# First pair's queries and the gates on ScalarE's queue, one transpose for the tails of keys and queries, and a new task order

## The chip, the core and the metric

One Trainium2 chip, one core. The metric is the device time of one execution of the whole program, in microseconds, as the median of several runs. A profiled execution gives the trace that is read below.

## What is computed

Attention with a memory, then two feed-forward layers, all in float32:

```
scores = q k^T / 8, causal; a = softmax(scores); local = a v            # B 4, H 8, S 576, D 64
q_p = phi(q) = max(q, 0) + exp(min(q, 0))
mem = (q_p M_prev) / (q_p . z_prev + 1e-6)
g = sigmoid(beta) per head;  x = g * mem + (1 - g) * local              # -> 2304 tokens x 512
x = (silu(x W_gate) * (x W_val)) W_out                                   # inner width 1536
out = m(x W_in) W_out2,  m = 0, h or (h + 1)^2 / 4 by the value of h     # inner width 2048
```

## The kernel before

Heads are taken two at a time: 16 pairs, numbered 0 to 15, four per batch. A pair's 576 positions are four chunks of 128 and a tail of 64. Each pair goes through the same tasks. Its keys (tile kn), queries (qn) and values (vn) are loaded; TensorE turns the keys (task tk for the chunks, tm for the tails of keys and queries) and the queries (tq); ScalarE copies the turned tiles from PSUM (to KK, SZ or SX, and QZ or Q4 for the tails). The scores of a head follow (qk0 and qk1 by head, qk4 for the tails of both heads, in two halves), VectorE takes mask and maximum (mx), ScalarE the exponential with its sum (ex), VectorE inverts the sums (sum, tile r), GpSimd scales the rows (.sc), TensorE turns them (t03, t02, t01, t4 for the first head and the tails, t13, t12, t11 for the second), ScalarE or VectorE copies them (R), and TensorE forms the products with the values and the memory (av00 to av11). Beside that runs the memory path: ScalarE's two passes over qn (tile e), VectorE's p, GpSimd's w, fold and pn, the turn tp and its copy PP. The result x is stored to a scratch tensor xs.

The pairs of the first batch use plain float32 matmuls. From pair 4 on each operand is split into a high and a low part; ScalarE writes the high part, VectorE the low one, and SyncE copies the turned keys to the other half of the partitions (task dup, KK<-KK), which the scores wait for.

In between, TensorE has filler work: 72 blocks of six matmuls (mm<-xh,wu) that already form the first layer's inner products for three groups of 512 tokens and six slices of 256 columns, as soon as their x and the decoded weights are there. Twelve units of weights are decoded in this part as well (raw, wA, wS, wu; ScalarE, VectorE and GpSimd). Their results go out as gvo.

The order of all this on each engine is fixed when the program is built. `Plan.order` is a list scheduler: each task has an engine, an estimated duration and a priority, and a free engine takes the ready task with the lowest priority for which buffers are free. For a pair's task the priority is 100 times the pair's number plus an entry of the table `ORDER`; `EARLY` holds the priorities of the weight units, `GROUP_AT` and `X_AT` those of the filler's groups and of their loads. PSUM has five banks for the attention and three for the filler. SyncE issues nearly all transfers, in order. From the end of the filler on, a second plan runs the two layers; its priorities are other numbers, which the change doesn't touch.

At the start, `Attention.__init__` builds masks, gates and zeroed tiles; `pair` then adds the tasks. The lines that matter are those of the loads (`l_k`, `l_q`), `tm` and its copies:

Of the kernel before, what the change touches and what calls it, by code (L numbers as in the profile page):

```python
# [18 lines left out]
P = 128  # L19
# [18 lines left out]
EARLY = (-695.6332, 2783.9892, 1285.5157, 4826.1976, -587.204, 1099.0329, 1783.7958, 812.7126, 3810.6396, 6743.5654, -296.1106, 490.4918)  # L38
# [4 lines left out]
GROUP_AT, X_AT = (38662.3623, 35325.2542, 46229.556), (412.8002, 381.1663, 182.3662)  # L43
# [16 lines left out]
    "load": -940.6324, "load_v": 203.5903, "load_z": -887.0432, "load_M": -747.8821, "tk": -333.4689, "tm":  # L60
    -812.4048, "tk.hi": -890.2619, "tm.hi": 1721.9097, "tq": 461.8326, "tq.hi": 1307.1915, "min": 1423.9267,
    "exp": 311.185, "phi": 204.0583, "w": -1122.4349, "fold": -293.9033, "nrm": -731.8656, "pn": 1733.8628,
# [9 lines left out]
    -1003.2927, "M_lo": 15.9112, "tk.lo": 391.3507, "tm.lo": -125.9973, "dup": -273.878, "tq.lo": 560.4026,  # L72
# [159 lines left out]
def c_tr(n):  # L232
    return 109 * n
# [39 lines left out]
class Attention:  # L273
# [3 lines left out]
    def __init__(self, ctx, tc, plan, q, k, v, M_prev, z_prev, beta, cst, xs):  # L277
# [17 lines left out]
        ac = self.ac  # L295
        self.mask0 = ac.tile([P, 512], F32, name="mask0")
# [12 lines left out]
        bb = ac.tile([P, H], F32, name="bb")  # L309
        nc.sync.dma_start(bb, beta.partition_broadcast(P))  # L310
# [35 lines left out]
        for t in self.kn + self.vn:  # L346
            nc.gpsimd.memset(t[64:128, 4], 0.0)
# [4 lines left out]
        for t in self.SZ + self.QZ + self.MZ:  # L352
            nc.gpsimd.memset(t, 0.0)

    def pair(self, b, n):
# [17 lines left out]
        def add(eng, dur, name, fn, deps=(), uses=(), port=False):  # L373
            t = pl.add(eng, dur, num * 100 + ORDER[name], fn, deps, uses, port=port)
            t["name"] = name
            return t

        def dma(name, times, fn, deps=(), uses=()):
            t = pl.dma(num * 100 + ORDER[name], times, fn, deps, uses)
            t["name"] = pl.last["name"] = name  # L380
            return t
# [34 lines left out]

        def tail_full(t, src):
            nc.sync.dma_start(t[:, 8, :], src.rearrange("h p d -> h p d"))
# [23 lines left out]
        def M_lo():  # L442
            nc.gpsimd.tensor_sub(st["Mhl"][:, :, 1, :], st["mraw"], f32(st["Mhl"][:, :, 0, :]))

        l_k = dma("load", [728, 728, 182], load(
            "kn", lambda: self.kn[i_k.slot], lambda t: t[:, 0:4], self.k, tail_half), uses=[i_k])
        l_q = dma("load", [728, 728, 182], load(
            "qn", lambda: self.ld.tile([P, 9, D], F32, name="qn", tag="qn"), lambda t: t[:, 0:8].rearrange("p (c h) d -> p c h d", h=2), self.q, tail_full),
            uses=[i_q])
# [36 lines left out]
        def tm():  # L486
            t = psum("tm", i_tm)
            nc.tensor.transpose(
                t[:, 0:128], st["kn"][:, 4].rearrange("p h d -> p (h d)"), self.ident)
            nc.tensor.transpose(t[0:64, 128:256], st["qn"][:, 8], self.ident)  # L490
# [9 lines left out]
        t_tm = add("PE", c_tr(2), "tm", tm, [l_k, l_q], [i_k, i_q, i_tm, i_Q4] + i_K)  # L500
# [8 lines left out]
        if exact_q:  # L509
            t_k = copies("tk", [(lambda: st["tk"], lambda: f32(mk_K(0)[:, 0, 0:512]), 512)], [t_tk], [i_tk, *i_K])  # L510
            t_Q4 = copies("tm", [(lambda: st["tm"][:, 0:64], lambda: f32(mk_K(0)[:, 0, 512:S]), 64)] + [
                (lambda h=h: st["tm"][up, 128 + h * 64:192 + h * 64], lambda h=h: QZ[halves[h], h], 64)
                for h in range(2)], [t_tm], [i_tm, i_Q4, *i_K])
            t_K = [[t_k, t_Q4]] * 2
        else:
            t_k = [split("tk", k_parts("tk", slice(0, 512), slice(0, 512), h), [t_tk], [i_tk, i_K[h]], 100) for h in range(2)]
            tails = [x for h in range(2) for x in k_parts("tm", slice(0, 64), slice(512, S), h)]
            for h, j in ((0, 0), (1, 3)):
                tails.append((lambda h=h: st["tm"][up, 128 + h * 64:192 + h * 64],
                              lambda j=j: Q4[up, j], lambda j=j: Q4[dn, j], 64))  # L520
# [859 lines left out]
```

## Time and profile before

| | |
|---|---|
| median of three runs | 1110.57 us (1105.44 to 1111.51) |
| the profiled execution | 1110.57 us, of which 1108.8 us are its span, first to last instruction |
| TensorE busy | 1076.6 us (97%), 5520 matmuls |
| VectorE, ScalarE, GpSimd busy | 756.6, 565.4, 257.0 us |
| last product of the attention part, next stage's first matmul | 347.4 us, 360.0 us |

A busy time is the union of an engine's instructions; matmuls are pipelined, so a matmul's duration is longer than the step from its start to the next one's. PEclk is the clock that TensorE was granted, as a share of 2.4 GHz. The idle time in brackets behind a row is what the engine stood still before it, and what ended that.

### The profile page before, as it was taken

What the parts mean: (1) busy time and instruction counts of PE and PEld (TensorE: products, weight loads), DVE (VectorE), ACT (ScalarE), POOL (GpSimd) and SP (SyncE); (2) the same over time, 40 slices, a digit from 0 to 9 for tenths busy, and PEclk for the clock granted to TensorE, in tenths of its full rate; (3) what the DMA queues carried; (4) which work ended last, traced back from release to release, by engine and by line L of the source; (5) the groups of instructions that cost most, each with busy time, mean ns of one, the idle gap of its engine ahead of it and who ended that gap; (6) DMA issues with size and microseconds to landing.
All of it is one profiled execution on the core that took longest, in us unless ns stands there. A gap on an engine that the chain in (4) does not pass through costs nothing.

```text
span 1108.8 us, 16480 instructions
## 1 busy us (share of the span) xinstructions
PE 1076.6 (97%) x5520; PEld 924.7 (83%) x5520; DVE 756.6 (68%) x1699; ACT 565.4 (51%) x1286; POOL 257.0 (23%) x325
## 2 busy tenths in 40 slices
PE   6997999999999999999999999999999999999998
PEld 4565788888888998888789997888888888889997
DVE  5688989888983788798945559999433443343433
ACT  6888889999884254544433334454222222222222
POOL 6898669666653000000000000000000000000000
PEclk9999999999999999999999999999999999999999
DMA  5567545765725889976635567361300110110000
GB/s 138 156 172 187 146 123 150 209 165 127 234 91 173 289 302 320 345 235 202 212 104 176 166 221 246 111 236 57 110 1 1 57 39 1 43 39 1 29 1 29
DMA packets 148325, 156.42 MB, mean 141 GB/s; under 512 B 70160, under 2 KB 109072, under 8 KB 148240
## 3 DMA queue, kind: packets, MB, share of 16 engines
q1 hardware_dynamic: 147664, 154.31, 44.8%
q8 instruction: 44, 0.72, 0.3%
q10 hardware_dynamic: 576, 1.05, 0.2%
q14 instruction: 41, 0.34, 0.1%
HBM read 105.78 MB, written 42.47 MB: 134 GB/s over the span
## 4 chain that ended last, share of the span: by engine, by line
PE 50%; DVE 1%; DMA 0%; issue 0%; ACT 0%; DVEq 0%
PE acc L1274 27%; PE mm L1036 23%; DMA ys<-yo 0%; DVE t L1238 0%; DVE h L1251 0%; DVE wA L956 0%; DVE t L1244 0%; DVE wu L984 0%; DVE wA L977 0%; ACT yo L1304 0%; DVE yo L1308 0%; DVE wS L961 0%; DVE wA L949 0%; DVE wA L952 0%; ACT oo L1340 0%
## 5 line engine op out<-in xcount | busy, mean ns | idle before, releaser
L1036 PE MATMUL mm<-xb,wu 128*128 128x512 f32 (+1 forms) x1968 | 410.7, 363 | 0.0
L1036 PEld LDWEIGHTS mm<-xb,wu 128*128 128x128 f32 x1968 | 357.4, 188 | 42.0 <-DVE t L1242 0.2
L1274 PE MATMUL acc<-wu,h 128*128 128x512 f32 x864 | 208.1, 390 | 0.0
L1274 PEld LDWEIGHTS acc<-wu,h 128*128 128x128 f32 x864 | 161.8, 188 | 32.3
L1248 ACT CAST h<-t 128x512 fp32r<-128x512 f32 (+1 forms) x140 | 80.9, 578 | 180.6 <-DVE t L1242 90.1
L1274 PE MATMUL acc<-h,wu 128*128 128x512 f32 (+1 forms) x720 | 152.6, 368 | 2.4 <-DVE h L1251 2.4
L1236 DVE SCALAR_TENSOR_TENSOR t<-t 128x512 f32<-128x512 f32 (+1 forms) x80 | 51.0, 638 | 146.9 <-ACT t L1230 146.9
L1274 PEld LDWEIGHTS acc<-h,wu 128*128 128x128 f32 x720 | 131.0, 188 | 20.5 <-DVE h L1251 3.7
L1251 DVE TENSOR_TENSOR h<-t,h 128x512 fp32r<-128x512 f32 (+1 forms) x140 | 89.0, 636 | 71.8 <-ACT h L1248 71.5
L1230 ACT ACTIVATE t<-mm,half 128x512 f32<-128x512 f32 (+1 forms) x80 | 51.5, 644 | 147.6 <-PE mm L1036 147.2
L1036 PE MATMUL mm<-xh,wu 128*128 128x512 f32 x432 | 115.0, 405 | 1.2 <-DMA xh<-xs 0.9
L755 POOL TENSOR_SCALAR a<-a,r,OGP 128x256 f32<-128x256 f32 (+3 forms) x144 | 96.1, 680 | 28.1 <-DVE r L746 9.7
L1036 PEld LDWEIGHTS mm<-xh,wu 128*128 128x128 f32 x432 | 77.4, 190 | 16.1 <-DMA xh<-xs 1.8
L677 ACT ACTIVATE a<-a,mn 128x128 f32<-128x128 f32 (+3 forms) x128 | 71.0, 558 | 12.7 <-DVE mn L670 12.3
L981 ACT CAST wu<-wA 128x512 fp32r<-128x512 f32 x64 | 39.7, 620 | 52.9 <-DVE wA L977 52.3
L944 ACT ACTIVATE wA<-raw 128x512 f32<-128x512 f32 x64 | 43.2, 675 | 45.3 <-DVE wu L984 20.6
L1082 ACT COPY gvo<-mm 128x512 f32<-128x512 f32 (+1 forms) x80 | 42.9, 544 | 41.3 <-PE mm L1036 40.9
L670 DVE CUSTOM_DVE_ANT_0 a<-s,mask 128x256 f32<-128x256 f32 (+3 forms) x128 | 57.7, 484 | 7.2 <-PE s L664 4.8
L397 DVE TENSOR_TENSOR R<-t,R 128x384 fp32r<-128x384 f32 (+3 forms) x120 | 53.3, 484 | 4.5 <-ACT R L393 3.7
L956 DVE SCALAR_TENSOR_TENSOR wA<-raw,wA 128x512 uint32<-128x512 uint32 x68 | 54.3, 801 | 0.6
L1242 DVE TENSOR_TENSOR t<-t,mm 128x512 f32<-128x512 f32 (+1 forms) x80 | 50.6, 632 | 2.2
L664 PE MATMUL s<-KK,SX 128*128 128x512 f32 (+3 forms) x192 | 42.0, 342 | 8.3 <-DMA KK<-KK 3.5
(134 smaller groups left out, 1401.5 us busy)
## 6 DMA issues: line engine op xcount, KB each, us to landing
raw<-in_moe_w_out_dram SPq DMA_DIRECT2D x28, 512.0 KB, 4.5
xb<-xs SPq DMA_DIRECT2D x24, 512.0 KB, 6.2
gv<-gv SPq DMA_DIRECT2D x24, 512.0 KB, 4.4
gv<-gvo SPq DMA_DIRECT2D x44, 256.0 KB, 4.6
xs<-x SPq DMA_DIRECT2D x16, 576.0 KB, 3.3
raw<-in_moe_w_in_dram SPq DMA_DIRECT2D x16, 512.0 KB
KK<-KK SPq DMA_DIRECT2D x24, 288.0 KB
raw<-in_moe_w_gate_dram SPq DMA_DIRECT2D x12, 512.0 KB, 4.7
```

The lines of the kernel that those rows point to most:

```text
L397: nc.vector.tensor_sub(lo(), src(), f32(hi()))
L670: nc.vector.tensor_tensor_reduce(a, st[f"s{h}{c}"][:, 0:kl], self.mask0[:, 512 - kl:512], -0.125, 3.0e38, ALU.add, ALU.min, mn[:, o:o + 1])
L677: nc.scalar.activation(a, a, AF.Exp, bias=mn[:, o:o + 1], scale=-1.0, accum_out=sm[:, o, 0:1])
L755: nc.gpsimd.tensor_scalar(a, a, st["mn"]["r"][:, o:o + 1], self.OGP[:, n, o:o + 1], op0=ALU.mult, op1=ALU.mult)
L956: nc.vector.scalar_tensor_tensor(s["F"], words(s["raw"])[:, :, 1], 0xC0000000, s["A"], op0=ALU.bitwise_and, op1=ALU.bitwise_or)
L1036: nc.tensor.matmul(out, kt_of(unit, pw, kt), x[kt][:, px, cols], start=(kt == 0 and i == 0), stop=(kt == KT - 1 and i == 2))
L1230: nc.scalar.activation(s["t"], src[0][0](), AF.Relu, bias=half, scale=0.5)
L1236: nc.vector.scalar_tensor_tensor(s["t"], s["t"], 1.0, s["t"], op0=ALU.min, op1=ALU.mult)
L1242: nc.vector.tensor_max(s["t"], s["t"], src[0][0]())
L1248: nc.scalar.copy(s["h"][:, 0], s["t"])
L1251: nc.vector.tensor_sub(s["h"][:, 1], s["t"], f32(s["h"][:, 0]))
L1274: nc.tensor.matmul(state[m][:, 0:o], l, r, start=(f == 0 and i == 0), stop=(f == F - 1 and i == 2), skip_group_check=True)
```

## The change

Five things change.

- The first pair's queries (three transfers) and the gates' vector `bb` are issued by ScalarE at the very start; before, SyncE issued them, `bb` ahead of the first keys.
- With each pair's keys the tail of its queries is loaded as well, into the 64 rows of `kn` that were zeroed before (`tail_two`, one more transfer for each pair). The query tile still gets its own copy of the tail, for the memory path.
- `tm` is one transpose of 128 x 128 in place of two, and no longer depends on the load of the queries. The copies read the queries' tail from columns 64 to 127; for a split pair the second head's high part now lies in the lower half of the partitions.
- The zeroing of SZ, QZ and MZ moves from GpSimd to VectorE, that of kn's unused rows goes.
- `ORDER`, `EARLY`, `GROUP_AT` and `X_AT` hold new numbers, so the tasks of the attention part stand in another order on every engine.

```diff
-EARLY = (-695.6332, 2783.9892, 1285.5157, 4826.1976, ...
+EARLY = (-287.4065, 1887.8432, 16137.615, 9256.0877, ...
-GROUP_AT, X_AT = (38662.3623, 35325.2542, 46229.556), (412.8002, 381.1663, 182.3662)
+GROUP_AT, X_AT = (20260.1724, 25727.3732, 55014.2119), (875.5215, -266.6973, -218.444)
...
-    "load": -940.6324, "load_v": 203.5903, "load_z": -887.0432, "load_M": -747.8821, "tk": -333.4689, "tm":
+    "load": -1161.5582, "load_v": 452.1889, "load_z": -1110.878, "load_M": 414.315, "tk": -2068.1283, "tm":
...
+        bb = ac.tile([P, H], F32, name="bb")
+        self.q0 = self.ld.tile([P, 9, D], F32, name="qn", tag="qn")
+        for h in range(2):
+            nc.scalar.dma_start(self.q0[:, 0:8].rearrange("p (c h) d -> p c h d", h=2)[:, :, h, :],
+                                q[0, h, 0:512, :].rearrange("(c p) d -> p c d", p=P))
+        nc.scalar.dma_start(bb, beta.partition_broadcast(P))
+        nc.scalar.dma_start(self.q0[:, 8, :], q[0, 0:2, 512:S, :].rearrange("h p d -> h p d"))
...
-        bb = ac.tile([P, H], F32, name="bb")
-        nc.sync.dma_start(bb, beta.partition_broadcast(P))
...
-        for t in self.kn + self.vn:
+        for t in self.vn:
             nc.gpsimd.memset(t[64:128, 4], 0.0)
...
-        for t in self.SZ + self.QZ + self.MZ:
-            nc.gpsimd.memset(t, 0.0)
+        for t in self.QZ + self.SZ + self.MZ:
+            nc.vector.memset(t, 0.0)
...
+        def tail_two(t, src):
+            tail_half(t, src)
+            nc.sync.dma_start(t[dn, 4], self.q[b, hs, 512:S, :].rearrange("h p d -> p h d"))
...
+        if near:
+            l_q = add("DMA", 1820, "load", lambda: st.update(qn=self.q0), [], [i_q])
+        else:
+            l_q = dma("load", [728, 728, 182], load(
...
-            nc.tensor.transpose(t[0:64, 128:256], st["qn"][:, 8], self.ident)
...
-        t_tm = add("PE", c_tr(2), "tm", tm, [l_k, l_q], [i_k, i_q, i_tm, i_Q4] + i_K)
+        t_tm = add("PE", c_tr(1), "tm", tm, [l_k], [i_k, i_tm, i_Q4] + i_K)
...
-                (lambda h=h: st["tm"][up, 128 + h * 64:192 + h * 64], lambda h=h: QZ[halves[h], h], 64)
+                (lambda h=h: st["tm"][halves[h], 64:128], lambda h=h: QZ[halves[h], h], 64)
```

How the engines' rows move, at three places. Lines of the new kernel are 11 to 12 higher behind the inserted code.

ScalarE, from its first instruction to its first exponential of scores, before (e is the memory path's pass over the queries, KK, QZ and SZ the copies that the first scores read):

```order
L313 ACT_TABLE_LOAD
L313 ACTIVATE gate<-bb 128x8
L316 ACTIVATE ogate<-bb 128x8
L505 COPY KK<-tk 128x512
L552 ACTIVATE e<-qn 128x576
L505 COPY KK<-tm 128x64
L505 COPY QZ_180<-tm 64x64 x2
L555 ACTIVATE e<-e 128x576
L505 COPY SZ_178<-tq 64x512 x2
L717 ACTIVATE a_0_170,sum_156<-a_0_170,mn 128x576
```

And now:

```order
L299 DMA qn<-in_q_dram 128x4x64 x2
L301 DMA bb<-in_beta_dram 128x8
L302 DMA qn<-in_q_dram 128x1x64
L318 ACT_TABLE_LOAD
L318 ACTIVATE gate<-bb 128x8
L321 ACTIVATE ogate<-bb 128x8
L563 ACTIVATE e<-qn 128x576
L516 COPY SZ_180<-tq 64x512
L566 ACTIVATE e<-e 128x576
L516 COPY SZ_180<-tq 64x512
L516 COPY KK<-tm 128x64
L516 COPY QZ_182<-tm 64x64 x2
```

Four transfers stand ahead of the table load, and the copy of the keys' chunks (KK<-tk), which was the first copy, is the last of them, behind the twelve rows shown.

TensorE in pair 7, before: the last twelve rows of the stretch from the turn of its keys (tk, with the seven rows of a product av00 behind it) to its first score (s<-KK,SX):

```order
L863 MATMUL av_2000<-R_1730,vhl 128x64
L533 MATMUL tq<-ident,qn 128x128 x4
L802 MATMUL t_2031<-ident,a_1743 128x128 x4
L802 MATMUL t_2040<-ident,a_1814 128x128 x4
L1036 MATMUL mm<-xh,wu 128x512 x6
L802 MATMUL t_2067<-ident,a_1871 128x128 x3
L819 MATMUL t_2073<-ident,a_1761 128x128
L819 MATMUL t_2073<-ident,a_1732 128x128 x2
L802 MATMUL t_2079<-ident,a_1812 128x128 x3
L1036 MATMUL mm<-xh,wu 128x512 x6
L664 MATMUL s_2100<-KK,SX 128x512 x2
L664 MATMUL s_2106<-KK,SX 128x384 x2
```

The same stretch now, from the turn of the tails on (tm, one row), its first twelve rows:

```order
L500 MATMUL tm<-ident,kn_171 128x128
L1047 MATMUL mm<-xh,wu 128x512 x6
L495 MATMUL tk<-ident,kn_171 128x128 x4
L602 MATMUL tp<-ident,p 128x128 x4
L605 MATMUL tp_1873<-ident,p 64x128
L813 MATMUL t_1881<-ident,a_1534 128x128 x3
L544 MATMUL tq<-ident,qn 128x128 x4
L1047 MATMUL mm<-xh,wu 128x512 x12
L675 MATMUL s_1937<-KK,SX 128x384 x2
L1047 MATMUL mm<-xh,wu 128x512 x6
L874 MATMUL av_1958<-PP,Mhl 128x256
L874 MATMUL av_1958<-R_1654,vhl 128x256
```

Behind these there follow the other three rows of that product, t4 (5 transposes), six filler matmuls, t01 (3 transposes) and a product of 256 columns, and then pair 7's first score; s_1937 is pair 6's. Twenty-four filler matmuls lie between the turn and the score, where there were twelve.

TensorE at the end of the attention part, before: the last product of pair 15, the filler behind it and the next stage (mm<-xb,wu):

```order
L863 MATMUL av_5070<-R_4968,vhl 128x64
L863 MATMUL av_5070<-R_4969,vhl 128x320 x3
L863 MATMUL av_5070<-R_4969,vhl 128x192
L863 MATMUL av_5070<-R_4969,vhl 128x64
L1036 MATMUL mm<-xh,wu 128x512 x54
L1036 MATMUL mm<-xb,wu 128x384 x384
```

And now:

```order
L813 MATMUL t_5071<-ident,a_4920 128x128 x3
L1047 MATMUL mm<-xh,wu 128x512 x12
L874 MATMUL av_5094<-PP,Mhl 128x320
L874 MATMUL av_5094<-R_5004,vhl 128x320 x3
L874 MATMUL av_5094<-R_5004,vhl 128x192
L874 MATMUL av_5094<-R_5004,vhl 128x64
L874 MATMUL av_5094<-R_5005,vhl 128x320 x3
L874 MATMUL av_5094<-R_5005,vhl 128x192
L874 MATMUL av_5094<-R_5005,vhl 128x64
L1047 MATMUL mm<-xh,wu 128x512 x36
L1047 MATMUL mm<-xb,wu 128x384 x384
```

Three of the nine filler blocks behind the last product have moved ahead of it.

## Rows read from the trace of the kernel before

**Rows 1.** The page's first line.

```profile
span 1108.8 us, 16480 instructions
```

**Rows 2.** Busy us of each engine by stretch (x: instructions), granted clock, DMA share, GB/s.

```profile
0.00:20.00 20.00, 13.18 (x56) 9.01 (x56) 10.01 (x46) 12.74 (x32) 13.38 (x38) 1.00 0.51 123
20.00:100.00 80.00, 73.24 (x379) 49.18 (x380) 61.92 (x178) 69.92 (x196) 70.43 (x76) 0.98 0.65 172
...
160.00:345.00 185.00, 181.08 (x1163) 160.67 (x1162) 160.24 (x486) 168.84 (x464) 129.48 (x161) 1.00 0.55 155
...
362.00:1108.80 746.80, 740.02 (x3542) 647.26 (x3540) 470.42 (x848) 261.18 (x459) 0.00 (x0) 1.00 0.40 132
```

**Rows 3.** Whom TensorE waited for, 20 to 345 us: total, times, longest.

```profile
PE s L664 <- DMA KK<-KK: 3.5, 3, 2.5
PE s L664 <- DVE mn L670: 3.1, 2, 2.9
PE av L863 <- ACT PP L505: 2.1, 1, 2.1
PE t L819 <- POOL a L755: 1.7, 1, 1.7
PE s L664 <- DVE R L397: 1.6, 2, 1.4
```

**Rows 4.** One of the three stretches at half clock, as in rows 2.

```profile
155.20:158.60 3.40, 3.40 (x11) 3.02 (x12) 2.06 (x9) 1.36 (x5) 0.01 (x1) 0.50 0.02 6
```

**Rows 5.** Timeline of SyncE's queue at the start: start, length, what.

```profile
4.15 0.64 SPq L418 DMA_DIRECT2D qn<-in_q_dram  x1
```

**Rows 6.** Timeline of ScalarE at the start.

```profile
7.33 0.68 ACT L552 ACTIVATE e<-qn 128x576 f32<-128x576 f32 x1 [1.09 <-DMA qn<-in_q_dram]
...
8.01 0.42 ACT L505 COPY QZ<-tm 64x64 f32<-64x64 f32 x2
...
9.04 1.17 ACT L505 COPY SZ<-tq 64x512 f32<-64x512 f32 x2
```

**Rows 7.** Timeline of TensorE at the start.

```profile
4.53 1.09 PE L483 MATMUL tk<-ident,kn 128*128 128x128 f32 x4 [4.53 <-DMA kn<-in_k_dram]
...
7.26 0.42 PE L490 MATMUL tm<-ident,qn 128*64 128x128 f32 x1 [1.43 <-DMA qn<-in_q_dram]
...
15.55 0.60 PE L533 MATMUL tq<-ident,qn 128*128 128x128 f32 x4
```

**Rows 8.** Timeline of TensorE in pair 7, turn of the keys and first score.

```profile
145.53 0.65 PE L483 MATMUL tk<-ident,kn 128*128 128x128 f32 x4
...
155.19 2.56 PE L664 MATMUL s<-KK,SX 128*128 128x512 f32 x8 [2.46 <-DMA KK<-KK]
```

**Rows 9.** End of the attention part: TensorE, SyncE, and the loads' median time to landing.

```profile
347.39 12.79 PE L1036 MATMUL mm<-xh,wu 128*128 128x512 f32 x54
360.02 3.31 PE L1036 MATMUL mm<-xb,wu 128*128 128x384 f32 x18
...
354.73 0.36 SPq L1110 DMA_DIRECT2D xb<-xs  x1
...
xb<-xs SPq DMA_DIRECT2D x16, 384.0 KB, 5.6
```

**Rows 10.** Timeline of TensorE in a regular pair, the turns of the tails.

```profile
249.44 0.27 PE L488 MATMUL tm<-ident,kn 128*128 128x128 f32 x1
249.55 0.27 PE L490 MATMUL tm<-ident,qn 128*64 128x128 f32 x1
249.58 0.39 PE L863 MATMUL av<-PP,Mhl 128*128 128x320 f32 x1
```

**Rows 11.** Timeline of TensorE, last scores and second head's first turn, pairs 11 and 7.

```profile
243.30 0.57 PE L664 MATMUL s<-KK,SX 128*128 128x256 f32 x4
...
251.54 0.60 PE L802 MATMUL t<-ident,a 128*128 128x128 f32 x4
...
171.85 0.42 PE L664 MATMUL s<-KK,SX 128*128 128x128 f32 x2
...
177.68 0.55 PE L819 MATMUL t<-ident,a 128*128 128x128 f32 x3 [0.54 <-DVE R L397]
```

More of the change, by code (lines that the diff above doesn't have):

```diff
@@ L37 @@
 CUTS = (0, 2, 4)
-EARLY = (-695.6332, 2783.9892, 1285.5157, 4826.1976, -587.204, 1099.0329, 1783.7958, 812.7126, 3810.6396, 6743.5654, -296.1106, 490.4918)
+EARLY = (-287.4065, 1887.8432, 16137.615, 9256.0877, -215.5057, 4250.8554, 811.5698, -202.2738, 4594.4235, 9367.785, 2548.5565, -122.2052)
 XH, GVO = 4, 3
@@ L59 @@
 ORDER = {
-    "load": -940.6324, "load_v": 203.5903, "load_z": -887.0432, "load_M": -747.8821, "tk": -333.4689, "tm":
-    -812.4048, "tk.hi": -890.2619, "tm.hi": 1721.9097, "tq": 461.8326, "tq.hi": 1307.1915, "min": 1423.9267,
-    "exp": 311.185, "phi": 204.0583, "w": -1122.4349, "fold": -293.9033, "nrm": -731.8656, "pn": 1733.8628,
[9 rows of a table removed]
-    -1003.2927, "M_lo": 15.9112, "tk.lo": 391.3507, "tm.lo": -125.9973, "dup": -273.878, "tq.lo": 560.4026,
[5 rows of a table removed]
+    "load": -1161.5582, "load_v": 452.1889, "load_z": -1110.878, "load_M": 414.315, "tk": -2068.1283, "tm":
+    -3489.133, "tk.hi": 1956.633, "tm.hi": 3325.5154, "tq": 1515.3186, "tq.hi": 58.9504, "min": 813.3241, "exp":
[10 rows of a table added]
+    "M_lo": 207.2265, "tk.lo": 630.5307, "tm.lo": -58.8903, "dup": -146.9326, "tq.lo": 1568.2686, "tp.lo":
[4 rows of a table added]
 }
@@ L443, in M_lo @@
             nc.gpsimd.tensor_sub(st["Mhl"][:, :, 1, :], st["mraw"], f32(st["Mhl"][:, :, 0, :]))
[L445 to L449, printed above, removed]
+        l_k = dma("load", [728, 728, 182, 182], load(
+            "kn", lambda: self.kn[i_k.slot], lambda t: t[:, 0:4], self.k, tail_two), uses=[i_k])
+        if near:
+            l_q = add("DMA", 1820, "load", lambda: st.update(qn=self.q0), [], [i_q])
+        else:
+            l_q = dma("load", [728, 728, 182], load(
+                "qn", lambda: self.ld.tile([P, 9, D], F32, name="qn", tag="qn"), lambda t: t[:, 0:8].rearrange("p (c h) d -> p c h d", h=2), self.q, tail_full),
+                uses=[i_q])
         l_v = dma("load_v", [728, 728, 182], load(
@@ L518, in pair @@
             for h, j in ((0, 0), (1, 3)):
-                tails.append((lambda h=h: st["tm"][up, 128 + h * 64:192 + h * 64],
-                              lambda j=j: Q4[up, j], lambda j=j: Q4[dn, j], 64))
+                tails.append((lambda h=h: st["tm"][halves[h], 64:128], lambda h=h, j=j: Q4[halves[h], j],
+                              lambda h=h, j=j: Q4[halves[1 - h], j], 64))
             t_Q4 = split("tm", tails, [t_tm], [i_tm, i_Q4] + i_K)
```

28 rows, old and new, of the table ORDER are left out of this document.

## Prediction

> **What bounds the kernel now.** I read the page first. The span is 1108.8 us [rows 1] inside an execution of 1110.57 us, which is also the median of the three runs, so the sum below is made on 1110.57 and needs no correction between the two. Then the table of stretches [rows 2]. From 362 us on TensorE is busy 740.0 of 746.8 us: it is the bound there, and the two programs hold the same instructions in the same order from that point. The time can therefore only change by moving the end of the attention part, some 360 us. In that part TensorE is busy 13.2 of the first 20 us, 73.2 of the next 80 and 181.1 of the 185 from 160 to 345; ScalarE is busy 168.8 of those 185. So two engines are nearly full, and a saved wait of TensorE is worth its length only while ScalarE keeps up.
>
> Third, who TensorE waits for after the first 20 us [rows 3]: the copy of the keys to the other half of the partitions (KK<-KK) 3.5 us in three waits, score banks that VectorE has not emptied (mn, R) 3.1 and 1.6, ScalarE's copy PP 2.1, the scaling on GpSimd 1.7. Fourth, the clock: after the longest such waits it is granted at 0.50, so at 1.2 instead of 2.4 GHz, for one stretch of 3.4 us [rows 4]; there are three of these (near 22, 111 and 155 us), each after TensorE had stood for 1.7 to 2.9 us. At half speed 3.4 us do the work of 1.7.
>
> **The change part by part.** *The first pair's queries on ScalarE's queue.* Before, their tail is the seventh transfer of SyncE's queue, issued at 4.15 for 0.64 us [rows 5], and TensorE sees it at 7.26 after waiting 1.43 us [rows 7]; it needs 2.5 us from the issue's end to use. In the new order ScalarE issues four transfers first. An issue costs 0.36 us (row of xb, [rows 9]) to 0.64; from about 0.7 us the tail is issued by 2.2 to 3.3 and there by 4.7 to 5.8. That looks like 1.5 to 2.5 us gained. But the copies that the scores need stand on ScalarE behind it in this order: e (0.68), a query copy, e again (0.68), the second query copy (1.17 for the two), the keys' tail and two tail copies (0.42 for the two, and a shorter one that I take at 0.2), the keys (0.58, as one of the two 512-column copies) [rows 6]: 3.7 us. The scores start at 8.4 to 9.5 plus hand-over. Before, the first transposes take 1.09 us for four and later ones 0.60 [rows 7], so the block of scores that ends at 15.55 begins at half speed, and an earlier start buys mostly slow time. I get an end of 15.2 to 16.1 against 15.55: 0, from -0.4 to +0.6. The gates land and are used under this as well, and the zeroing moves from GpSimd to VectorE, which has no other work before the gates: 0, hidden by the same 3.7 us; without that cover each of the two 1024-column zeroings, the widest of it, would cost some 1.2 us (estimated by columns from the 512-column copies at 0.58).
>
> The Trainium skill ("Trainium Kernel Development and Optimization", Key Constraints) says that DMAs of all issuing queues run on the same 16 engines and interleave, so that issuing from several engines saves only the sequencer's issue time. No row shows two queues at work together here. By that rule the gain at the start is at most some issues of SyncE; by the row of SyncE's tail alone it could be the whole 1.43 us wait. The sum takes neither: ScalarE's own queue of copies ends last.
>
> *One transpose for both tails.* Sixteen transposes go. In a full stretch the one of the queries takes 0.03 us of TensorE's time (249.55 to 249.58), the one of the keys 0.11 (249.44 to 249.55) [rows 10]. So 0.5 to 1.8 us, and I take 1.2. The added SyncE issue per pair costs 0.64 us [rows 5], 15 times 0.64 = 9.6 us of a queue; SyncE mostly waits for buffers ahead of these, and the transpose no longer waits for the whole query tile, so I take 0 here and price the other case below.
>
> *The new order: keys.* The scores of a pair from number 4 on wait for ScalarE's and VectorE's copies and the transfer KK<-KK. In pair 7 TensorE starts the transposes of the keys at 145.53, has work for 7.2 us and waits 2.46 us, until 155.19 [rows 8]: this stretch needs 9.7 us. In the new order there stand between the same two points 24 filler matmuls at 12.63 / 54 = 0.234 us (347.39 to 360.02, [rows 9]) = 5.6; 24 transposes (tk 4, tp 5, t12 3, tq 4, t4 5, t01 3) at 0.11 [rows 10] = 2.6; one score of two times 384 columns and two products of 1024 columns each, at 0.234 for 512, = 0.35 and 0.95. That is 9.5 us, so 0.2 of the 2.46 stay. For pairs 8 to 13 the same count gives 6.7 to 13.9 us of work where before it was 6.1 to 6.6, so the small waits there close too. Of 3.5 us of waits and 1.7 of half clock I take 4.2 as gained; the bounds are 0 and 5.2.
>
> *The new order: the rest.* Pair 3's memory queries were turned right ahead of the products that use them, which is the 2.1 us of PP [rows 3]; now three groups of pair 4's scores, some 1.3 us, stand between: -2.0, from -2.1 to 0. Waits for banks: five banks as before, in another order: 0, from -4.7 to +4.7 (their 3.1 and 1.6 gone, or once more). On the other side some products stand closer behind their last turn than any before (about 0.7 to 1.3 us of work in pairs 1, 3 and 4): +1.5, from 0 to +4.2 (twice the row of PP).
>
> *The end of the attention part.* Before, 54 filler matmuls stand behind the last product, 12.63 us [rows 9]. The last x is stored under them, the load of its part issues at 354.73 and lands 5.6 us later (the median of such loads), 360.3; it is first needed after 15 matmuls of the next stage, about 15 x 0.234 x 384 / 512 = 2.6 us after 360.02, so 2.3 us are spare. Now 36 filler matmuls are left: 18 x 0.234 = 4.2 us less cover. 4.2 - 2.3 = +1.9, from 0 to +4.2.
>
> Sum: 0 - 1.2 - 4.2 - 2.0 + 0 + 1.5 + 1.9 = -4.0, and **1110.57 - 4.0 = 1106.6 us**. The single bounds added up would be far wider than anything likely, since they are independent; three quarters of each end about give -8 and +4 for this case, 1102.5 to 1114.5.
>
> **The rivals.** *Faster by more:* the waits for banks go as well, and with no wait over 1.7 us no half-clock stretch comes. For it: these waits stand next to those of the keys, and the keys' chain gets 2 to 7 us more cover. Price: the five rows of [rows 3] sum to 12.0, of which two thirds go, 8.0; two more stretches of half clock, 3.4; transposes 1.2; against that half of the 1.9 + 1.5 above: -10.9, 1099.7 us. Against it: ScalarE's 168.8 of 185 us leaves at most 16 us in the whole stretch.
>
> *Slower:* the chain of the second head's softmax loses its cover. Place: from a pair's last score to the first turn of the second head, through VectorE, ScalarE, VectorE and GpSimd. Before, a regular pair has 8.2 us between them, 243.30 to 251.54, and no wait at the end [rows 11]. In the new order eight of the twelve later pairs have 4.3 to 6.2 us of TensorE's work there. If the chain needs its 8.2, they lose about 2.5 us each, 20 us, less the 5.4 of transposes and keys: +14.6, 1125 us. Against it: pair 7 had only 5.8 us, 171.85 to 177.68, and waited 0.54 for a bank, not for GpSimd [rows 11]. It decides from a need of about 6.5 us on. A smaller form of the same side: SyncE's 9.6 us of added issues fall on the path of the keys: 1110.57 - 4.0 + 9.6 = 1116.2.
>
> *Nothing that can be measured moves:* the waits close, and ScalarE, 91% busy, ends last instead, so that only the transposes and the end count: 1110.57 - 1.2 + 1.9 = 1111.3.
>
> **How the numbers follow.** Chances: the forecast 0.40, faster by more 0.32, softmax chain 0.13, SyncE's issues 0.06, nothing moves 0.09. A measurement here tells about 0.5% from no change, so 1105.0 to 1116.1 counts as the same. The forecast's own range reaches below 1105.0 with some 0.06 of its chance: faster 0.32 + 0.06 = 0.38. Slower: 0.13 and most of the 0.06 = 0.18. Same: the rest, 0.44. The range holds 8 in 10: from 1095, a little under the faster rival, to 1117, which leaves out most of the softmax chain.
>
> **What would show it.** Right: KK<-KK and PP all but gone from TensorE's waits, two or fewer stretches at 0.50, the block of first scores ending between 15 and 16.5 us, the next stage's first matmul near 356 us. Wrong: waits of turns for GpSimd in pairs 7 to 13 (softmax), keys' loads issued later on SyncE (issues), or a first stage at the same 360 us with other waits.

## The result

The changed kernel takes 1121.15 us (median, 1118.11 to 1124.29) against 1110.29 us for the kernel before in the same comparison (1105.44 to 1111.51): a ratio of 1.0106, 95% interval 1.0086 to 1.0126. It is slower by some 11 us, where I had forecast 1106.6 us and a range that ends at 1117.

The profiled execution is 1121.25 us, with this span:

```profile
span 1119.5 us, 16437 instructions
```

Busy us by stretch, after (columns as in [rows 2]: TensorE, its weight loads, VectorE, ScalarE, GpSimd, then clock, DMA share, GB/s):

```profile
0.00:20.00 20.00, 12.42 (x43) 8.00 (x43) 11.43 (x51) 11.67 (x30) 7.53 (x27) 1.00 0.48 108
20.00:100.00 80.00, 72.58 (x373) 49.03 (x373) 64.76 (x176) 69.01 (x191) 71.54 (x81) 0.98 0.64 171
100.00:160.00 60.00, 56.60 (x342) 47.22 (x342) 53.34 (x158) 56.17 (x150) 45.75 (x52) 1.00 0.59 165
160.00:345.00 185.00, 172.79 (x1071) 152.15 (x1070) 151.28 (x454) 158.69 (x434) 118.44 (x152) 0.97 0.54 150
367.00:1119.50 752.50, 743.48 (x3556) 649.63 (x3554) 469.53 (x848) 261.82 (x461) 0.00 (x0) 1.00 0.40 133
```

The stretch from 100 to 160 us of the kernel before, which the rows ahead of the prediction left out:

```profile
100.00:160.00 60.00, 52.08 (x302) 43.93 (x301) 52.60 (x139) 47.90 (x128) 42.25 (x51) 0.94 0.52 147
```

Up to 160 us the new order keeps its promise: from 100 on TensorE is busy 56.6 us where it was 52.1, at full clock. From 160 to 345 it loses more than that, 172.8 against 181.1 us [rows 2], and ScalarE falls from 168.8 to 158.7: no engine is full there, work stands and waits. Over 20 to 345 us TensorE is idle 325 - 302.0 = 23.0 us, before 325 - 306.4 = 18.6. The next stage's first matmul comes at 367.62, 7.6 us later than before [rows 9]. Idle time makes 5.2 of the 7.6: the 4.4 just named, and 0.8 in the first 20 us. The other 2.4 fit work at lower speed (an estimate, from durations given below): the first scores take 1.4 us longer, and 3.4 us more at half clock are worth 1.7, less the transposes saved. The rest of the run takes 3.1 us more as well, 2.2 of it idle time of TensorE (752.5 - 743.5 = 9.0 us, before 746.8 - 740.0 = 6.8).

Whom TensorE waited for from 20 to 345 us, after (total, times, longest), beside [rows 3]:

```profile
PE mm L1047 <- DMA xh<-xs: 4.2, 3, 3.7
PE s L675 <- DMA KK<-KK: 2.3, 4, 0.9
PE t L813 <- DVE mn L681: 2.0, 1, 2.0
PE av L874 <- DVE R L402: 1.6, 3, 0.8
PE s L671 <- DVE R L777: 1.4, 1, 1.4
PE s L675 <- DVE xf L886: 1.4, 2, 0.8
PE tq L544 <- ACT SZ L516: 1.3, 1, 1.3
PE av L874 <- DVE PP L402: 1.2, 3, 0.7
```

KK<-KK and PP are smaller, as forecast, but the list is longer: xh<-xs, the filler's own input (before 0.9 us, 0.6 at the longest), stands first, and many waits of about 1 us are new (R from L777 is the copy of a turned tile, xf a product that VectorE takes out of its bank). Up to the next stage there are three stretches at half clock, 13.6 us in all against three of 3.4, 10.2 us, before [rows 4]. The second and the third come behind the waits for mn and xh:

```profile
22.50:25.90 3.40, 3.21 (x14) 2.45 (x15) 2.50 (x4) 2.99 (x9) 3.40 (x5) 0.50 0.60 132
176.50:183.30 6.80, 6.54 (x24) 5.87 (x25) 4.97 (x19) 5.47 (x16) 2.19 (x3) 0.53 0.39 120
305.90:309.30 3.40, 3.40 (x15) 3.29 (x14) 1.77 (x7) 0.61 (x2) 1.17 (x3) 0.51 0.20 77
```

The double length of the second is not the new order's own: `x4_order` below, under the same order, is at 0.50 there from 181.05 to 184.46 us, 3.4 us, and `x3_queue`, under the old order, from 110.2 to 117.0, 6.8 us.

### The profile page after: what moved, and what is told of

Read it like the earlier page. It is cut to its first block, busy times and chain, and to the rows that moved or that the text cites. A ratio compares the mean times of both kernels' runs of the same rounds, so it can differ in the third digit from the quotient of the medians.

```text
span 1119.5 us, 16437 instructions
## 1 busy us (share of the span) xinstructions
PE 1079.9 (96%) x5504; PEld 925.0 (83%) x5504; DVE 759.1 (68%) x1705; ACT 568.9 (51%) x1286; POOL 251.4 (22%) x317
## 4 chain that ended last, share of the span: by engine, by line
PE 47%; DVE 3%; DMA 1%; issue 0%; ACT 0%; SPq 0%; DVEq 0%; ACTq 0%
PE acc L1285 25%; PE mm L1047 22%; DMA raw<-in_moe_w_in_dram 1%; DVE t L1249 0%; DVE h L1262 0%; DVE wS L975 0%; DVE t L1255 0%; DVE wA L967 0%; DVE wu L995 0%; DVE wS L972 0%; DVE yo L1319 0%; DVE wA L988 0%; DVE wA L960 0%; DVE wA L963 0%; ACT wA L955 0%
## 5 line engine op out<-in xcount | busy, mean ns | idle before, releaser
L766 POOL TENSOR_SCALAR a<-a,r,OGP 128x256 f32<-128x256 f32 (+3 forms) x144 | 95.1, 673 | 19.4 <-DVE r L757 15.2
L688 ACT ACTIVATE a<-a,mn 128x384 f32<-128x384 f32 (+3 forms) x128 | 71.5, 561 | 11.9 <-DVE mn L681 11.3
L681 DVE CUSTOM_DVE_ANT_0 a<-s,mask 128x128 f32<-128x128 f32 (+3 forms) x128 | 59.2, 485 | 18.7 <-PE s L675 10.0
L967 DVE SCALAR_TENSOR_TENSOR wA<-raw,wA 128x512 uint32<-128x512 uint32 x68 | 49.5, 730 | 0.6
L675 PE MATMUL s<-KK,SX 128*128 128x256 f32 (+3 forms) x192 | 43.6, 342 | 5.5 <-DMA KK<-KK 2.3
```

Source lines behind the costliest of these rows:

```text
L681: nc.vector.tensor_tensor_reduce(a, st[f"s{h}{c}"][:, 0:kl], self.mask0[:, 512 - kl:512], -0.125, 3.0e38, ALU.add, ALU.min, mn[:, o:o + 1])
L688: nc.scalar.activation(a, a, AF.Exp, bias=mn[:, o:o + 1], scale=-1.0, accum_out=sm[:, o, 0:1])
L766: nc.gpsimd.tensor_scalar(a, a, st["mn"]["r"][:, o:o + 1], self.OGP[:, n, o:o + 1], op0=ALU.mult, op1=ALU.mult)
L967: nc.vector.scalar_tensor_tensor(s["F"], words(s["raw"])[:, :, 1], 0xC0000000, s["A"], op0=ALU.bitwise_and, op1=ALU.bitwise_or)
```

## The experiments

**How order and structure were kept apart.** Any edit of a task's duration or of its rests (what it has to wait for, as the planner is told) makes the planner draw another order. So most kernels here give the planner the durations, rests and numbers of one kernel and emit the instructions of the other; every task then stands exactly where it stood. Ratios are to the kernel before, with 95% intervals:

| kernel | order | ratio | interval |
|---|---|---|---|
| the changed kernel | new | 1.0106 | 1.0086 to 1.0126 |
| x4_order: new order alone | new | 1.0123 | 1.0104 to 1.0141 |
| x1_struct: structure alone | old | 1.0053 | 1.0032 to 1.0074 |
| x2_tails: one transpose with its load | old | 1.0077 | 1.0061 to 1.0092 |
| x3_queue: ScalarE's queue at the start | old | 1.0004 | 0.9990 to 1.0019 |
| x6_issue, x14_issue2: added load, not read | old | 1.0056, 1.0051 | 1.0040 to 1.0072, 1.0029 to 1.0074 |
| x17_two: the same load in two issues | old | 1.0088 | 1.0067 to 1.0108 |
| x7_noload: one transpose, no load | old | 1.0019 | 1.0007 to 1.0032 |
| x12_late: one transpose, pairs 4 to 15 | old | 1.0051 | 1.0032 to 1.0071 |
| x13_late_q: x12 with ScalarE's queue | old | 1.0059 | 1.0040 to 1.0078 |
| x16_gpq, x18_late_gpq: x12, x13, load by GpSimd | old | 1.0098, 1.0079 | 1.0070 to 1.0125, 1.0058 to 1.0100 |
| x19_after_gpq: changed kernel, load by GpSimd | new | 1.0136 | 1.0113 to 1.0159 |
| x9_xlast, x11_start: one or two tasks moved | new | 1.0134, 1.0112 | 1.0113 to 1.0154, 1.0094 to 1.0131 |
| x15_replan: structure, old numbers | third | 1.0182 | 1.0154 to 1.0209 |
| x20_zh: before, zh in one load | old | 0.9981 | 0.9969 to 0.9993 |
| x21_struct_zh: x1 with zh in one load | old | 1.0054 | 1.0034 to 1.0074 |

**Structure or order?** Theory: the new order costs the time. Rivals: SyncE's added issues, or ScalarE's start. `x4_order` has the edits of `x1_struct` the other way round.

```diff
 # x1_struct: the planner sees the load that it saw before, the emitted code is the changed one
-            "kn", lambda: self.kn[i_k.slot], lambda t: t[:, 0:4], self.k, tail_half), uses=[i_k])
...
+            "kn", lambda: self.kn[i_k.slot], lambda t: t[:, 0:4], self.k, tail_two), uses=[i_k])
+        if near:
+            l_q = dma("load", [728, 728, 182], lambda: st.update(qn=self.q0), uses=[i_q])
...
```

> The new order alone: loads, tails and zeros as before, under the planner's durations and numbers of the changed kernel, so that the tasks stand in exactly the order of the changed kernel. If the new order alone costs the time: 1118 to 1123 us (1.007 to 1.012), with the wait of group 2's filler for its x near 305 us and half-clock stretches near 176 and 305 us. If structure costs it: 1107 to 1112 us, without these two stretches.

> The whole change of structure (first queries and gates by ScalarE's queue, zeros of SZ, QZ and MZ by VectorE, key and query tails in one transpose) under the order of before: the planner is given the old durations, rests and numbers, so that the tasks stand in exactly the old order. If the new order alone costs the time: 1107 to 1111 us (ratio 0.997 to 1.000: one transpose less is worth up to 1.2 us). If SyncE's fifteen added issues and the longer loads of keys cost it: 1116 to 1121 us (1.005 to 1.010), with waits for doubled keys (KK<-KK) that are longer than before. If ScalarE's start costs it: 1112 to 1114 us, and all of it before the 20th us.

> The one transpose alone (query tails loaded twice, the second time into the upper rows of the keys' tile) under the order of before. My prediction's term: -1.2 us, from -1.8 to -0.5, with the fifteen added issues on SyncE at 0: 1108 to 1110 us. The rival on SyncE's issues: 1116 us (1.005). The theory that the order costs all of it: within 1108 to 1111.

> The first pair's queries and the gates by ScalarE's queue alone, and the zeros of SZ, QZ and MZ by VectorE, under the order of before. My prediction's term: 0 (-0.4 to +0.6), the first scores end between 15.2 and 16.1 us: 1110 to 1111 us. If the start of the changed kernel costs time whatever the order: 1112 to 1113 us (its first scores began 1.1 us later than before, and the second pair's transposes 2.6 us later).

The new order alone costs more than the whole change, 1.0123; the queue costs nothing that can be told; but the one transpose with its load costs 0.77% by itself, so two theories hold at once. They do not add up: 1.0053 and 1.0123 would make 1.018, and the changed kernel is at 1.0106. `x1_struct` lies in the range given to SyncE's issues, but the sign named with it, longer waits for KK<-KK, did not come in its profiled execution (2.8 us, before 3.5). The order-only kernel, by stretch:

```profile
100.00:160.00 60.00, 55.56 (x338) 45.91 (x337) 51.94 (x151) 53.42 (x142) 43.26 (x51) 1.00 0.57 157
160.00:345.00 185.00, 173.03 (x1079) 152.20 (x1078) 152.56 (x458) 159.21 (x438) 120.06 (x153) 0.98 0.54 150
```

It has most of the gain from 100 to 160 us and the same loss behind it, without any of the new loads. The fall of ScalarE from 169 to 159 us is the order's too.

**The one transpose: load or turn?** A square of four: with or without the added load, with one transpose or two.

```diff
 # x6_issue, x14_issue2 (without kn's zeroing): the two transposes stay    # x17_two: one load for each head
+            nc.sync.dma_start(t[dn, 4], self.q[b, hs, 512:S, :].rearrange("h p d -> p h d"))
 # x7_noload: the second transpose goes, no load is added
-            nc.tensor.transpose(t[0:64, 128:256], st["qn"][:, 8], self.ident)
```

> The kernel before with the added load alone: the tails of the queries are also loaded into the upper rows of the keys' tile (one more issue on SyncE for each pair, ahead of the loads of the queries), but the two transposes stay as they were and nobody reads those rows. The one-transpose kernel under the old order took 1.0077 of before. If the added issue on SyncE is what costs it: 1.007 to 1.010 (1116 to 1119 us). If it is the new rests of the transpose or its copies: 0.999 to 1.001.

> The added load alone again (both transposes kept, nobody reads the rows), but without GpSimd's zeroing of these rows: in the first such kernel the first added load had to wait for that zeroing (3.79 instead of 2.97 us), and its first scores began 1.0 us later than in the one-transpose kernel. If the added issue alone makes the cost: 1.004 to 1.006 (1112.5 to 1115 us), first scores near 9.5 us. If that zeroing made it: 1.000 to 1.002.

> The one transpose under the order of before without the added load: the upper rows of the keys' tile stay zero, so the tails of the queries are left out of the scores (the tail rows of the output differ). If the added issue on SyncE is the cost of the tails: 0.997 to 1.000 (1105 to 1108 us), the 1.2 us that my prediction gave to the saved transposes. If the cost is in the transpose and its copies: 1.006 to 1.009.

> As x14_issue2 (the added load alone, 1.0051), with the load cut into one for each head: the same bytes and packets, two added issues of SyncE per pair instead of one. If each issue costs its time: about twice as much, 1.009 to 1.011 (1117 to 1120 us). If the transfer costs: 1.004 to 1.006, unchanged.

The load that nobody reads costs 0.51 to 0.56%, some 6 us (I had expected 0.7 or more), with GpSimd's zeroing of its rows or without; the one transpose without it costs 0.19% rather than gaining 0.1%. Together that is 0.70 to 0.75%, near the 0.77% of `x2_tails`. The same bytes in two issues cost 0.88%: by the middle values the issue costs, not the transfer, though the intervals overlap. In the first 33 us SyncE issues without a pause, and the added issues shift all of it. The last values of the start in its queue, before:

```profile
31.00 1.23 SPq L409 DMA_DIRECT2D vn<-in_v_dram  x2
```

and in `x2_tails`:

```profile
34.76 1.14 SPq L409 DMA_DIRECT2D vn<-in_v_dram  x2
```

The same values are issued 3.8 us later. The Trainium skill ("DMA: Bandwidth & Descriptors", Issuing engines are not separate DMA queues) calls the sequencer's time for an issue usually small beside the transfer. For one transfer the trace agrees (0.61 us against a median of 2.8 us to landing for these loads, in the changed kernel); but in a row that is never idle, as here up to 33 us, each issue delays all that stand behind it.

**Only at the start?**

```diff
 # x12_late, x13_late_q: pairs 0 to 3 keep the two transposes and have no added load
+            "kn", lambda: self.kn[i_k.slot], lambda t: t[:, 0:4], self.k, tail_half if exact_q else tail_two), uses=[i_k])
...
-            nc.tensor.transpose(t[0:64, 128:256], st["qn"][:, 8], self.ident)
+            if exact_q:
+                nc.tensor.transpose(t[0:64, 128:256], st["qn"][:, 8], self.ident)
```

> The one transpose and the added load for pairs 4 to 15 alone, under the order of before; pairs 0 to 3 keep their two transposes. In the trace of before SyncE issues without a pause from 0.7 to 32.9 us, and with the added issues everything in it is up to 3 us later (the last v of the start 32.9 against 36.5 us). If the added issues cost where SyncE is never idle, at the start: 1.000 to 1.003 (1108 to 1111 us). If they cost in every pair, in the way of the keys' copies: 1.005 to 1.008, nearly all of the 1.0077.

> As x12_late, and the first queries and the gates by ScalarE's queue: the parts of the change without the issues that are added at the start, under the order of before. If the start was the cost and ScalarE's queue gives its 0.7 us of earlier scores: 0.998 to 1.001, at best a little faster than before. If the added issues cost all along: 1.004 to 1.007, like the whole structure (1.0053).

No: 0.51% stay without the start, two thirds of the 0.77% by the middle values. My theory of the busy start explains the other third at most.

**Another queue.**

```diff
 # x16_gpq against x12_late, x18_late_gpq against x13_late_q, x19_after_gpq against the changed kernel, for pairs 4 to 15
-            nc.sync.dma_start(t[dn, 4], self.q[b, hs, 512:S, :].rearrange("h p d -> p h d"))
+            nc.gpsimd.dma_start(t[dn, 4], self.q[b, hs, 512:S, :].rearrange("h p d -> p h d"))
```

> As x12_late (one transpose and the added load for pairs 4 to 15, order of before, 1.0051), with the added load issued by GpSimd's queue instead of SyncE's: the same bytes move, SyncE has no added issue. If SyncE's place in the row costs: back to 0.999 to 1.002 (1107 to 1110 us), the 1.0019 of the kernel without the load at most. If the transfer itself costs (bytes and packets in the DMA engines): 1.004 to 1.006, as x12_late.

> As x13_late_q (pairs 4 to 15 in one transpose, first queries by ScalarE's queue, order of before, 1.0059), with the added load by GpSimd's queue. If SyncE's issues were the cost: 0.998 to 1.001, the version that could beat before. If the transfers were: 1.004 to 1.006.

> The changed kernel with the added load of pairs 4 to 15 issued by GpSimd's queue. Its order alone cost 1.0123 with no added issue, so if the new order carries the whole cost by itself: 1.009 to 1.012 (1117 to 1121 us), unchanged. If it is SyncE's added issues that stand behind its late transfers (x of the second group, KK<-KK): 1.003 to 1.006 (1111 to 1114 us).

Neither expectation came in any of the three. All are slower than their partners by the middle values, so they do not tell issue from transfer: the issue now stands in GpSimd's own row (0.63 us each), and GpSimd is busy 70 of the 80 us from 20 to 100 [rows 2]. `x16_gpq`, GpSimd (three rows of an unbroken row of work), then VectorE, then TensorE, in an execution that is 5 us above the median of its runs:

```profile
58.10 0.63 POOL L419 DMA_DIRECT2D kn<-in_q_dram  x1
58.78 0.77 POOL L760 TENSOR_SCALAR a<-a,r,OGP 128x512 f32<-128x512 f32 x1
...
65.63 1.25 POOL L989 TENSOR_TENSOR wu<-wA,wu 128x512 fp32r<-128x512 f32 x1
```

```profile
60.75 6.32 DVE L584 SCALAR_TENSOR_TENSOR nrm<-nrm,GP 128x9 f32<-128x9 f32 x1
```

```profile
68.38 1.65 PE L665 MATMUL s<-KK,SZ 128*128 128x256 f32 x4 [4.54 <-DVE x L397]
```

An operation on nine columns stands 6.32 us on VectorE while GpSimd works without a gap; all scores behind it wait, and TensorE 4.54 us.

**Can single waits of the new order be taken away?** The largest one comes from SyncE's row in the changed kernel. The last part of the second group's x (xh) needs the store of pair 11's x (xs), and it is issued 7.6 us behind it. The first row is that store in the kernel before, the others are the changed kernel:

```profile
282.94 0.56 SPq L904 DMA_DIRECT2D xs<-x  x1
...
290.53 0.41 SPq L915 DMA_DIRECT2D xs<-x  x1
291.35 1.98 SPq L414 DMA_DIRECT2D qn<-in_q_dram  x2
...
298.15 0.38 SPq L1121 DMA_DIRECT2D xh<-xs  x1
298.63 1.13 SPq L535 DMA_DIRECT2D KK<-KK  x2
```

```profile
305.26 1.20 PE L1047 MATMUL mm<-xh,wu 128*128 128x512 f32 x3 [3.65 <-DMA xh<-xs]
```

```diff
 # x9_xlast: the load of xh directly behind the store that it needs
+        o = self.order()
...
+            o.insert(1866, o.pop(1906))
...
 # x11_start: the first pair's keys first, on TensorE and on ScalarE
+            o.insert(4, o.pop(13))
+            o.insert(5, o.pop(17))
```

> The changed kernel with one task moved: SyncE loads the last part of the second group's inputs (xh) directly behind the store that it needs, ahead of the last pair's queries, z and the rest, not 7.6 us later. In the changed kernel's trace TensorE waits 3.65 us for it near 305 us and then runs 3.4 us at half clock. If such waits of the new order add up to its cost: 3.65 and 1.7 us less, 1116 us (1.005). If TensorE would be held up later anyway, or the wait is handed on: 1120 to 1122 us (1.009 to 1.011).

> The changed kernel with the first pair's keys first again: their transposes ahead of those of the queries on TensorE, and their copy ahead of the others on ScalarE, as the old order has them. In the changed kernel the first scores wait 2.04 us for that copy, which stands last on ScalarE, and begin at 9.68 us, against 7.80 with the same loads under the old order. If the order of these copies sets the start: the first scores begin near 8.0 us and the whole is 1.0 to 1.7 us shorter, 1119.5 us (1.009). If the start is hidden behind later waits: 1121 us (1.0105), though the first scores begin early.

`x9_xlast` is no faster, 1.0134, above both of its ranges. Its queue of SyncE and the wait of TensorE:

```profile
293.49 0.41 SPq L918 DMA_DIRECT2D xs<-x  x1
299.22 0.36 SPq L1124 DMA_DIRECT2D xh<-xs  x1
299.69 2.28 SPq L417 DMA_DIRECT2D qn<-in_q_dram  x2
...
305.06 1.12 SPq L538 DMA_DIRECT2D KK<-KK  x2
```

```profile
309.39 0.82 PE L712 MATMUL s<-KK,Q 128*128 128x288 f32 x2 [4.11 <-DMA KK<-KK]
```

The load of xh now holds SyncE for 5.3 us until the store has landed; the keys' copy behind it is late instead, and TensorE waits 4.11 us for that. The filler's wait comes not from a misplaced load alone: pair 11's x itself is finished later under the new order, its store issued at 290.5 us, before at 282.9. `x11_start` does what it should at the start, from 9.68 to the first row here; the second is the next stage's first matmul:

```profile
7.80 7.11 PE L675 MATMUL s<-KK,SZ 128*128 128x512 f32 x16 [0.66 <-ACT SZ L520]
...
365.73 2.80 PE L1051 MATMUL mm<-xb,wu 128*128 128x384 f32 x15
```

and the whole is at 1.0112, not to be told from 1.0106. In the profiled execution the next stage begins 1.9 us earlier too (367.62 in the changed kernel), so there the gain is not lost on the way; but 1.9 us are 0.17%, less than these intervals tell, and whether the kernel keeps them is not shown. They would be a small part of the 11 us.

**Do the old numbers help?** `x15_replan` is the changed kernel with the four tables of numbers of before.

> The changed kernel with the planner's numbers of before (EARLY, GROUP_AT, X_AT, ORDER), so that the planner makes a third order out of the old numbers and the new rests. If the new numbers are what is bad, the old ones give 1110 to 1114 us (1.002 to 1.005, near the old order with this structure, 1.0053). If an order is only as good as its fit to the very structure that it was made for, a third order costs at least as much as the new one: 1119 us or more (1.009 and up).

1.0182, the slowest of all. The numbers behind the old order, the better of the two that were tried with the old structure, give the worst one with the new.

**An issue less.**

```diff
 # x20_zh, x21_struct_zh
-            for h in range(2):
-                nc.sync.dma_start(st["zh"][h * 64:(h + 1) * 64], self.z[b, 2 * n + h].partition_broadcast(64))
+            z = self.z[b, hs]
+            nc.sync.dma_start(st["zh"], bass.AP(tensor=z.tensor, offset=z.offset, ap=[[D, 2], [0, 64], [1, D]]))
```

> The kernel before with one issue less per pair: the two loads of z for the tails (zh, one for each head, 0.57 us each on SyncE) become one of the same bytes; nothing else, the same order. If each issue of SyncE costs what the added ones did (1.0051 and 1.0056 for the first sixteen, 0.35% more for the next sixteen): 0.995 to 0.997 (1101 to 1104 us), faster than both kernels. If the added issues cost because any shift disturbs an order that was fitted to the old times: 1.000 to 1.004.

> The whole change of structure under the order of before (x1_struct, 1.0053) with the same merged load of zh, so that SyncE has as many issues per pair as before, or fewer at the start. If SyncE's issues were the cost: 0.999 to 1.002 (1106 to 1109 us). If an order's fit is what counts: 1.004 to 1.008, no better than x1_struct.

One issue less per pair makes the kernel before faster by 0.19% (0.07 to 0.31), about a third of what one more costs and between the two expectations; it is faster than both kernels. Under the changed structure the same edit gains nothing. So neither theory takes all: an issue of SyncE has a price, but most of what the structure costs under the old order is not bought back by issues. That the old order was fitted to the old times is the reading that is left. It is argued, not shown: the profiled executions of `x1_struct` and `x21_struct_zh` are each the fastest of their runs (spans 1108.7 and 1107.8 us), and don't show where the median's 6 us go.

## Why the prediction was wrong

**The step that failed** is the price of the new order: keys -4.2, PP -2.0, banks 0, short covers +1.5 and the end +1.9, together -2.8 us. `x4_order` measures that order alone, with the old code, at some +13.5 us (1.0123). The prediction took the waits of the old trace one by one and counted every matmul that moved in ahead of them as cover that is ready when its turn comes. What the moved work itself needs, above all the filler's x, got no term. A second step failed too, the added issue at 0, though under the new order its cost can't be seen. Why the costs of order and structure do not add up stays open.

**The bound** was read rightly in the main: the end of the attention part moves the time. 7.6 of the 10.7 us of span are lost ahead of 367.62; the other 3.1 come behind it, which I had put at nothing because the second program's order is the same.

**The queries on ScalarE's queue: 0.** Right under the old order, 1.0004: the first scores even begin earlier, at 7.80 against 8.57 us. Under the new order ScalarE's chain of copies ends last, as the prediction said, and takes 3.5 us (forecast 3.7):

```profile
6.13 0.69 ACT L563 ACTIVATE e<-qn 128x576 f32<-128x576 f32 x1 [0.43 <-DMA qn<-in_q_dram]
...
9.04 0.58 ACT L516 COPY KK<-tk 128x512 f32<-128x512 f32 x1
```

```profile
9.68 7.52 PE L671 MATMUL s<-KK,SZ 128*128 128x512 f32 x16 [2.04 <-ACT KK L516]
17.04 1.14 PE L704 MATMUL s<-KK,QZ 128*128 128x288 f32 x4
```

The scores start only after the last of it, and the block of both rows ends at 18.1, not at 15.2 to 16.1. It begins 1.1 us later than before and lasts 8.4 us instead of 7.0: the sixteen products behind SZ take 7.4 us, before 4.9. So this term is +2.5 us at that place; what it is worth at the end is not shown (`x11_start`).

**One transpose: -1.2.** Wrong in sign, +2 us (`x7_noload`). **The added issue: 0.** The premise was "SyncE mostly waits for buffers ahead of these". It costs 6 us under the old order, of the size of the rival that I gave 0.06 (9.6 us, for fifteen issues; there are sixteen). Under the new order the structure makes no difference that can be told (1.0106 with it, 1.0123 without).

**Keys, -4.2, and PP, -2.0.** These came in the main. Pair 7's first score waits 0.56 us where it waited 2.46:

```profile
146.74 0.47 PE L675 MATMUL s<-KK,SX 128*128 128x256 f32 x2 [0.56 <-DMA KK<-KK]
```

There is no half clock between 100 and 160 us, and TensorE is busy 4.5 us more there. The waits for KK<-KK went from 3.5 to 2.3 us, and the half clock behind pair 7's, worth 1.7, is gone: 2.9 of the 4.2. Pair 3's wait for PP, 2.1 us, is gone, with 0.6 us for a copy R in its place.

**Banks, 0, and short covers, +1.5.** Scores and turns that wait for a copy of something they do not read, and so for a bank, sum to some 8 us before and some 10 now, over all rows of the two lists. Products close behind the copies that they read (av behind R and PP) wait 3.8 us, 2.8 of them in the rows shown above; before, pair 3's PP was the only one. Both terms lie within their bounds, on the slow side.

**The end, +1.9.** Measured 0.24 us:

```profile
359.18 8.61 PE L1047 MATMUL mm<-xh,wu 128*128 128x512 f32 x36
367.62 2.80 PE L1047 MATMUL mm<-xb,wu 128*128 128x384 f32 x15
370.66 1.51 PE L1047 MATMUL mm<-xb,wu 128*128 128x384 f32 x7 [0.24 <-DMA xb<-xs]
```

**What was missing** is a term for the filler's own input: 4.2 us of waits for xh, before 0.9, and a stretch at half clock behind the longest. I counted the filler as cover, 24 matmuls here and 36 there, and never asked whether its x would be there; its chain runs from a pair's last product over a store and SyncE's row. The idle time and the slower work account for the 7.6 us in one profiled execution. But the two runs that move single tasks, `x9_xlast` and `x11_start`, bring no gain that can be told, so which of these waits makes the cost of the order is not shown. The softmax rival did not come: TensorE waits 1.3 us in all for GpSimd's scaling, before 2.5. Nor did the condition of the faster rival, no half clock without a wait over 1.7 us: the stretch from 22.5 us stands behind waits of 1.26 and 0.69.

**The forecast's own range** holds a slip besides: three quarters of the terms' bounds, added up, are -10.7 and +9.9 us, not -8 and +4. The top would then be 1120.5 us, just below the 1121.15 measured.

## What to carry to other kernels

Measure an edit of the code and a new order apart, by holding the plan still: here each alone cost time (1.0053 and 1.0123), and the old numbers on the new code cost most (1.0182). That an order belongs to the durations and rests it was found with would explain this, but is not shown. When an order is priced by cover, ask of each piece of cover whether its own inputs will be there. An issue on a queue that many transfers share is not free just because the queue often waits; look for transfers that one issue can make, as zh's two (0.9981). And a wait taken from one transfer of an in-order queue can go to the next one behind it, as the keys' copy showed.

## What the runs showed of the hardware

VectorE's operations with two inputs in SBUF can stand beside a busy GpSimd for much longer than one of its instructions. In the kernel before, VectorE's step of the weights (median 0.69 us, longest 4.17):

```profile
107.24 3.12 DVE L956 SCALAR_TENSOR_TENSOR wA<-raw,wA 128x512 uint32<-128x512 uint32 x1
```

GpSimd worked without a gap beside it:

```profile
106.64 0.82 POOL L755 TENSOR_SCALAR a<-a,r,OGP 128x576 f32<-128x576 f32 x1
107.43 1.27 POOL L977 TENSOR_TENSOR wA<-wA,wS 128x512 f32<-128x512 f32 x1
108.66 1.15 POOL L585 TENSOR_TENSOR p<-p,nrm 128x576 f32<-128x576 f32 x1
```

VectorE ends 0.55 us after the last of them, the scores behind it are drained late, and this is where TensorE's longest wait for mn in [rows 3] comes from:

```profile
110.89 1.30 PE L664 MATMUL s<-KK,SX 128*128 128x256 f32 x4 [2.85 <-DVE mn L670]
```

In `x16_gpq` the 6.32 us above is the same (median of that line 0.17), and the changed kernel's wait of 2.0 us for mn follows on a step of the weights that took 1.81 us, from 174.28. The Trainium skill ("SBUF — State Buffer", Who interferes with whom) says that such an instruction and one of GpSimd that reads SBUF exclude each other, whichever comes first holding on for its whole instruction. The traces agree, and add that VectorE can lose to a whole row of them. The evidence is the timing; no run here takes GpSimd's row away.
